# Linformer attention and a max-of-three FFN on one core: sums and AV in 64x32 array tiles, w rows permuted, six attention groups, stores on the Pool queue, first batch turned on TensorE

## Chip, cores, metric

One core of one Trainium2 chip. The metric is device time of the kernel in microseconds (us), the median of its runs. Most runs of one kernel agree within 0.3%. A trace gives the span (first to last instruction), which is about 1.8 us shorter than the time of the same run.

## The reference, cut

Eight batches, eight heads, 1024 positions, head size 64. Keys and values are projected from 1024 positions to 64 (E and F), softmax attention runs over these 64, and the result goes through an FFN whose hidden value is the maximum of three products.

```python
k_proj = np.einsum('ks,bhsd->bhkd', E, k)            # E: 64 x 1024
v_proj = np.einsum('ks,bhsd->bhkd', F, v)
scores = scale * np.matmul(q, k_proj.transpose(0, 1, 3, 2))
attn = np.exp(scores - max); attn = attn / (sum(attn) + 1e-09)
x = np.matmul(attn, v_proj)  # transposed and reshaped to (8192, 512)
h = np.maximum(np.maximum(x @ w1, x @ w2), x @ w3)   # 512 -> 768
out = h @ w_out                                      # 768 -> 512
```

## The kernel before

The FFN of batch b runs as one long stream on TensorE; the attention of batch b+1 is cut into groups that are put between the FFN's matmul groups at fixed places ("slots": a slot is one group of 4 matmuls of the first layer, or one of 6 of the second). The data moves like this: the Pool queue loads k, v, q of a batch (cast to bf16 on the way); the Sync (SP) queue turns q and the projected k (kp) by DMA transpose and also issues the stores of the output.

```python
NB = 2                                        # two buffers of k, v, q, qT, kp2, kpT
def load(b, src, dst):                        # two DMAs of 512 KB, Pool queue
    ...
def q_turn(b):
    nc.sync.dma_start_transpose(out=qT[b % NB]..., in_=q_t[b % NB]...)

def attention(b):
    def kv(lo, hi): ...                       # 16 matmuls 128x64, two column halves at once
    def kv_out():
        kv(SI // 2, SI)
        nc.scalar.copy(out=kp2[i][:, :, 0, :], in_=kv_k)
        nc.vector.tensor_copy(out=kp2[i][:, :, 1, :], in_=kv_k)
        nc.sync.dma_start_transpose(out=kpT[i], in_=kp2[i]...)
        ...                                   # two copies of v
    def scores(u): ...                        # 8 matmuls in 64x64 tiles, 2 exp of 128x1024
    def av(g):                                # two heads: 4 matmuls for sums, 4 for AV, 64x64 tiles
        ...
        nc.scalar.activation(out=lns[n2], in_=ps[:, AB + 2:AB + 4, :], func=AF.Ln)
        nc.scalar.activation(out=rinv[n2], in_=lns[n2], func=AF.Exp, scale=-1.0)
        nc.vector.tensor_tensor(out=xT[b % 3][:, g, :, :], in0=ps[:, AB:AB + 2, :], in1=rinv[n2]..., op=ALU.mult)
    # slots: kv 1 and 3, scores(0) 10, av(0) 14, av(1) 19, scores(1) 24, av(2) 29, av(3) 34

load(0, k, k_t); load(0, v, v_t); load(0, q, q_t)
...                                           # three w, w_out, on the Pool queue too
q_turn(0)
for _, g in attention(0): g()
load(1, k, k_t); load(1, v, v_t); load(1, q, q_t)
q_turn(1)
for b in range(B):
    if b + 2 < B:
        load(b + 2, k, k_t); load(b + 2, v, v_t); load(b + 2, q, q_t)
    for ch in range(2):
        ...                                   # 18 slots of layer 1; 4 slots of layer 2 of the half before,
                                              # a store on nc.sync after each second of these
    if b + 2 < B:
        q_turn(b + 2)
```

The loads of batch b+2 stand in loop b, but the Pool queue has nothing else to do. So it issues a load as soon as the buffer is free, which is when kv of the batch two before has read it. In loop b that starts the loads of batch b+3 right behind the kv of batch b+1.

The softmax here doesn't subtract the row's maximum and nothing guards it: scores larger than these inputs give would overflow.

## Time and profile before

| | before |
|---|---|
| time, median of 2 runs | 484.77 us |
| span of the profiled run | 481.2 us |
| TensorE busy, share of the span | 82% |
| first FFN matmul starts | 75.9 us |
| loop periods, loops 0 to 5 (first kv matmul to that of the next loop) | 49.1, 54.1, 52.5, 50.7, 52.1, 47.6 us |
| kpT, issue to landing (min/median/max) | 2.5/8.6/16.8 us |

First the page's slices, 40 of 12 us each: busy tenths of TensorE, its granted clock in tenths, busy tenths of the DMA engines, and what these moved.

```profile
PE   1300038699979999899979997999999999999996
PEclk9955557899988999899999998999999999999999
DMA  8999997941698046911696159815111511111122
GB/s 128 208 200 196 198 198 128 191 81 44 135 195 164 8 140 111 222 58 44 149 214 132 44 132 186 174 45 131 57 44 45 131 57 44 45 44 45 44 79 96
```

For the first six slices (72 us) TensorE is nearly idle and the DMA engines are full at about 200 GB/s. After that TensorE is nearly full, with dents in the slices where the DMA is busy.

The chain of waits, in order of time (start, duration, what), says what fills the first 75 us:

```profile
6.69 15.14 DMA q_t<-in_q_dram
21.91 19.61 SPq L74
41.58 16.78 DMA kpT<-kp
58.40 1.10 PE ps L113 x8
```

q of batch 0 lands at 21.8 us, the transpose of q then occupies the SP queue for 19.6 us, and only behind it the transpose of kp can go, which lands at 58.4 us. Then come 17 us of attention with nothing to overlap it.

In the loops: the timeline of loop 2 (start, duration, engine, line, operation, out<-in, count; in brackets the idle time before and what ended it).

```profile
184.82 1.48 POOL L71 DMA_DIRECT2D k_t<-in_k_dram  x2 [49.51 <-PE ps L90]
185.91 1.43 SPq L99 DMA_TRANSPOSE kpT<-kp  x1
...
194.66 1.02 PE L113 MATMUL ps<-qT,kpT 64*64 64x512 bf16 x8 [3.13 <-DMA kpT<-kp]
...
199.03 1.89 PE L156 MATMUL ps<-xT,w_sb 128*128 128x512 bf16 x7
...
200.85 0.41 PE L130 MATMUL ps<-pT,ones 64*64 64x512 bf16 x4
...
201.09 0.39 PE L130 MATMUL ps<-pT,vp 64*64 64x512 bf16 x4
...
201.41 1.04 PE L156 MATMUL ps<-xT,w_sb 128*128 128x512 bf16 x4
```

Two readings. The loads (184.82) begin just before the transpose of kp (185.91), which lands only at 194.6; the scores wait 3.13 us for it. And a group of eight tile matmuls takes from 200.85 to 201.41, 0.56 us, two slots of 0.2155 us (the spacing of the FFN's matmuls) and the rest switching; with 0.1 us ahead of it, 0.65 us.

The stall costs more than its idle time. The windows of 2 us over that stall (us; then busy time of PE, PEld, DVE, ACT, POOL with counts; granted clock, DMA share, GB/s):

```profile
192.00:194.00 2.00, 0.00 (x0) 0.00 (x0) 0.34 (x1) 0.00 (x0) 0.00 (x0) 1.00 1.20 191
194.00:196.00 2.00, 1.33 (x9) 0.28 (x10) 0.00 (x0) 0.27 (x1) 0.00 (x0) 0.69 1.16 248
196.00:198.00 2.00, 2.00 (x6) 0.76 (x5) 0.46 (x1) 1.67 (x2) 0.00 (x0) 0.50 1.14 267
```

After the idle time the clock is 0.50: six matmuls run in these 2 us, where eleven do at full clock (202 to 204 us of the same trace).

How slow the transpose of kp is, from the view of the tile kpT (durations on the queue, and issue to landing):

```profile
L99 SPq DMA_TRANSPOSE kpT<-kp x8: 1195/1467/6355, 41.6 to 388.7; - x8
DMA to landing us min/median/max: 2.5/8.6/16.8
```

The 2.5 us are of loops 5 and 6, in which no loads run any more, and these have no stall.

### The profile page before, as it was taken

The page shows a single profiled execution, that of the slowest core. Times are in us where ns is not written, and L with a number is a line of the kernel's source. Part 1 is how long each engine was busy: PE and PEld are TensorE (multiplying, and loading weights), DVE is VectorE, ACT ScalarE, POOL GpSimd, SP SyncE. Part 2 cuts the span into 40 slices and gives each one's busy share as a digit, 9 for nine tenths or more (in the row PEclk, how much of TensorE's full clock was granted, in tenths as well). Part 3 has the DMA queues.
Part 4 walks back from the last instruction along what each step waited for, and adds up shares of the span by engine and source line. Part 5 has one row for each costly group of instructions (what it writes and reads, how often), then busy time and mean ns, then how long its engine had stood idle before and what let it go on. Part 6 is the DMA issues. An engine that isn't in the chain of part 4 may idle for free.

```text
span 481.2 us, 5204 instructions
## 1 busy us (share of the span) xinstructions
PE 394.6 (82%) x2025; PEld 163.4 (34%) x2064; DVE 181.4 (38%) x243; ACT 197.3 (41%) x273; POOL 40.6 (8%) x60
## 2 busy tenths in 40 slices
PE   1300038699979999899979997999999999999996
PEld 1100012233423443344434442444444444344442
DVE  0100023354423554254425352454445444453331
ACT  1000064255435633455246623554465446542222
POOL 7311101200120003000200003000000000000000
PEclk9955557899988999899999998999999999999999
DMA  8999997941698046911696159815111511111122
GB/s 128 208 200 196 198 198 128 191 81 44 135 195 164 8 140 111 222 58 44 149 214 132 44 132 186 174 45 131 57 44 45 131 57 44 45 44 45 44 79 96
DMA packets 73977, 55.13 MB, mean 115 GB/s; under 512 B 38752, under 2 KB 65632, under 8 KB 73952
## 3 DMA queue, kind: packets, MB, share of 16 engines
q0 software_dynamic: 27872, 28.58, 36.1%
q1 hardware_dynamic: 46080, 26.22, 20.0%
q8 instruction: 16, 0.26, 0.2%
q14 instruction: 9, 0.07, 0.0%
HBM read 57.15 MB, written 16.78 MB: 154 GB/s over the span
## 4 chain that ended last, share of the span: by engine, by line
PE 73%; DMA 16%; SPq 4%; ACT 2%; DVE 2%; POOL 1%; issue 1%; DVEq 0%; POOLq 0%
PE ps L156 49%; PE ps L168 16%; DMA kpT<-kp 13%; SPq L74 4%; PE ps L130 4%; DMA q_t<-in_q_dram 3%; PE ps L88 3%; PE ps L113 2%; ACT pT L118 1%; DVE xT L136 1%; DVE kp L98 1%; ACT kp L97 1%; ACT rinv L135 0%; ACT lns L134 0%; POOL v_t L71 0%
## 5 line engine op out<-in xcount | busy, mean ns | idle before, releaser
L156 PE MATMUL ps<-xT,w_sb 128*128 128x512 bf16 x1127 | 269.2, 385 | 2.0 <-issue 0.5
L156 PEld LDWEIGHTS <-w_sb 128*128 128x128 bf16 x1152 | 110.2, 99 | 148.9 <-issue 25.8
L161 DVE TENSOR_TENSOR m<-ps,h1s 128x512 f32<-128x512 f32 x96 | 66.2, 690 | 114.7 <-PE ps L156 114.4
L168 PE MATMUL ps<-wo_sb,hT 128*128 128x512 bf16 x370 | 94.1, 385 | 0.7
L159 ACT COPY h1s<-ps 128x512 f32<-128x512 f32 x96 | 56.1, 584 | 61.8 <-PE ps L156 61.8
L136 DVE TENSOR_TENSOR xT<-ps,rinv 128x1024 bf16<-128x1024 f32 x32 | 39.2, 1225 | 109.5 <-ACT rinv L135 109.5
L163 DVE TENSOR_TENSOR hT<-ps,m 128x512 bf16<-128x512 f32 x96 | 66.3, 691 | 35.5 <-PE ps L156 27.6
L170 ACT COPY o_acc<-ps 128x512 f32<-128x512 f32 x64 | 37.4, 584 | 75.0 <-PE ps L168 74.8
L118 ACT ACTIVATE pT<-ps 128x1024 bf16<-128x1024 f32 x32 | 31.0, 1021 | 68.4 <-PE ps L113 68.4
L113 PE MATMUL ps<-qT,kpT 64*64 64x512 bf16 x128 | 12.2, 462 | 55.7 <-DMA kpT<-kp 54.3
L168 PEld LDWEIGHTS <-hT 128*128 128x128 bf16 x384 | 37.1, 99 | 49.5 <-issue 8.8
L134 ACT ACTIVATE lns<-ps 128x1024 f32<-128x1024 f32 x32 | 32.8, 1024 | 25.5 <-PE ps L130 25.5
L135 ACT ACTIVATE rinv<-lns 128x1024 f32<-128x1024 f32 x32 | 33.8, 1057 | 1.0
L71 POOL DMA_DIRECT2D k_t<-in_k_dram x16 | 11.9, 750 | 224.7 <-PE ps L90 213.1
L113 PEld LDWEIGHTS <-kpT 64*64 64x64 bf16 x128 | 2.6, 112 | 63.4 <-DMA kpT<-kp 57.7
L88 PE MATMUL ps<-k_t,eT 128*64 128x512 bf16 x64 | 19.1, 427 | 6.1 <-DMA k_t<-in_k_dram 6.1
L90 PE MATMUL ps<-v_t,fT 128*64 128x512 bf16 x64 | 18.9, 427 | 4.4 <-DMA v_t<-in_v_dram 4.4
L97 ACT CAST kp<-ps 64x512 bf16<-64x512 f32 x8 | 4.6, 579 | 41.8 <-PE ps L90 41.8
L130 PE MATMUL ps<-pT,ones 64*64 64x512 bf16 x128 | 14.0, 427 | 5.5 <-ACT pT L118 4.1
L130 PE MATMUL ps<-pT,vp 64*64 64x512 bf16 x128 | 13.5, 407 | 3.4 <-DVE xT L136 3.4
L98 DVE CAST kp<-ps 64x512 bf16<-64x512 f32 x8 | 5.5, 683 | 21.0 <-ACT kp L97 21.0
L71 POOL DMA_DIRECT2D q_t<-in_q_dram x16 | 12.1, 771 | 14.8 <-DMA qT<-q_t 8.1
(25 smaller groups left out, 53.5 us busy)
## 6 DMA issues: line engine op xcount, KB each, us to landing
out_dram<-o_acc SPq DMA_DIRECT2D x32, 512.0 KB, 2.7
k_t<-in_k_dram POOLq DMA_DIRECT2D x16, 512.0 KB, 8.4
v_t<-in_v_dram POOLq DMA_DIRECT2D x16, 512.0 KB, 13.0
q_t<-in_q_dram POOLq DMA_DIRECT2D x16, 512.0 KB, 16.6
w_sb<-in_moe_w_dram POOLq DMA_DIRECT2D x3, 768.0 KB, 21.8
wo_sb<-in_moe_w_out_dram POOLq DMA_DIRECT2D x1, 768.0 KB, 27.7
e_sb<-in_E_dram POOLq DMA_DIRECT2D x1, 128.0 KB, 3.1
f_sb<-in_F_dram POOLq DMA_DIRECT2D x1, 128.0 KB, 3.1
```

Source lines behind the costliest of these rows:

```text
L88: nc.tensor.matmul(out=ps[0:KP, AB, :], lhsT=eT[:, si, :], rhs=k_t[i][:, :, si, :], start=(si == 0), stop=(si == SI - 1))
L118: nc.scalar.activation(out=pT[:, 4 * u + 2 * h2:4 * u + 2 * h2 + 2, :], in_=ps[:, AB + 2 * h2:AB + 2 * h2 + 2, :], func=AF.Exp, scale=scale)
L130: nc.tensor.matmul(out=ps[col * D:(col + 1) * D, AB + 2 * (1 - what) + par, :], lhsT=ones[rows, :] if what == 0 else vp2[i][rows, h, :], r ...
L134: nc.scalar.activation(out=lns[n2], in_=ps[:, AB + 2:AB + 4, :], func=AF.Ln)
L135: nc.scalar.activation(out=rinv[n2], in_=lns[n2], func=AF.Exp, scale=-1.0)
L136: nc.vector.tensor_tensor(out=xT[b % 3][:, g, :, :], in0=ps[:, AB:AB + 2, :], in1=rinv[n2].rearrange("p (c n) -> p c n", c=2), op=ALU.mult)
L156: nc.tensor.matmul(out=ps[:, bank, :], lhsT=w_sb[i][:, ct, jt * P:(jt + 1) * P], rhs=xT[b % 3][:, ct, ch, :], start=(ct == 0), stop=(ct == ...
L159: nc.scalar.copy(out=h1s[jt % 2], in_=ps[:, bank, :])
L161: nc.vector.tensor_tensor(out=m12[jt % 2], in0=ps[:, bank, :], in1=h1s[jt % 2], op=ALU.max)
L163: nc.vector.tensor_tensor(out=hT[c % 2][:, jt, :], in0=ps[:, bank, :], in1=m12[jt % 2], op=ALU.max)
L168: nc.tensor.matmul(out=ps[:, bank, :], lhsT=hT[c % 2][:, jt, tt * P:(tt + 1) * P], rhs=wo_sb[:, jt, :], start=(jt == 0), stop=(jt == NJT - 1))
L170: nc.scalar.copy(out=o_acc[c % 2][:, tt, :], in_=ps[:, bank, :])
```

## The change

The intent: fewer TensorE and ACT passes in sums and AV (TensorE's array split into eight tiles of 64x32, four heads of one parity at once, so the sums of all heads are made once and two of four Ln/Exp pairs fall away; w's rows are permuted to fit the new order of x); six attention groups instead of eight; stores moved off the SP queue, and q's transpose moved into the middle of the loop, so that the transposes don't queue behind stores; the first batch's q and kp turned on TensorE to start the FFN earlier.

```diff
-    def attention(b):
+    def attention(b, turn):
...
-        groups.append((1, lambda: kv(0, SI // 2)))
-        groups.append((3, kv_out))
...
+        def quads(lhs):
+            for par in range(2):
+                for g in range(NPAIR):
+                    for u in range(2):
+                        rows = slice(u * KP, (u + 1) * KP)
+                        nc.tensor.matmul(out=ps[g * HD:(g + 1) * HD, AB + 2 * u + par, :],
+                                         lhsT=lhs(rows, g), rhs=pT[rows, g, par, :], start=True, stop=True,
+                                         tile_position=(u * KP, g * HD))
+        def sums():
+            quads(lambda rows, g: ones[rows, :])
+            ...                                  # 2 Ln and 2 Exp of 128x1024
+        def av(half):
+            quads(lambda rows, g: vp2[i][rows, g, half * HD:(half + 1) * HD])
+            ...                                  # 2 multiplications into xT
+        return [(2, kv), (10, lambda: scores(0)), (15, lambda: scores(1)), (20, sums),
+                (25, lambda: av(0)), (30, lambda: av(1))]
+    def turn_pe(i):                              # 8 transposes on TensorE, one copy
...
-            nc.sync.dma_start(out=out_v[b, ch]...
+            nc.gpsimd.dma_start(out=out_v[b, ch]...
...
-        nc.gpsimd.dma_start(out=wt, in_=w.rearrange("(ct p) j -> p ct j", p=P))
+        wv = w.rearrange("(j c p) n -> j p c n", j=NPAIR, c=NCT)
+        for j in range(NPAIR):
+            nc.gpsimd.dma_start(out=wt[j * HD:(j + 1) * HD], in_=wv[j])
...
-    q_turn(0)
-    for _, g in attention(0):
+    for h in range(H):                           # 32 transposes of 128x128 on TensorE, 8 copies
+        ...
+    for _, g in attention(0, turn_pe):
...
+            if slot == 16 and b + 2 < B:
+                q_turn(b + 2)
...
-        if b + 2 < B:
-            q_turn(b + 2)
```

More of the change, by code (lines that the diff above doesn't have):

```diff
@@ L25 @@
     NCT, NJT = DM // P, DF // P
+    NPAIR = H // 2
     scale = 1.0 / float(D) ** 0.5
@@ L37 @@
     ident = T([P, P], BF16, "ident")
-    ones = T([P, KP], BF16, "ones")
+    ones = T([P, D // 2], BF16, "ones")
     e_sb = T([KP, S], BF16, "e_sb")
@@ L52 @@
     kpT = [T([P, H, KP], BF16, f"kpT{i}") for i in range(NB)]
-    vp2 = [T([P, H, D], BF16, f"vp2_{i}") for i in range(NB)]
-    pT = T([P, H, 512], BF16, "pT")
+    vp2 = [T([P, NPAIR, D], BF16, f"vp2_{i}") for i in range(NB)]
+    pT = T([P, NPAIR, 2, 512], BF16, "pT")
     xT = [T([P, NCT, 2, 512], BF16, f"xT{i}") for i in range(3)]
@@ L80, with kv @@
     AB = 4
-    def attention(b):
+    HD = D // 2
+    def attention(b, turn):
         i = b % NB
-        groups = []
-        def kv(lo, hi):
-            for si in range(lo, hi):
+        def kv():
+            for si in range(SI):
                 nc.tensor.matmul(out=ps[0:KP, AB, :], lhsT=eT[:, si, :], rhs=k_t[i][:, :, si, :],
@@ L91, in kv @@
                                  start=(si == 0), stop=(si == SI - 1))
-        def kv_out():
-            kv(SI // 2, SI)
             kv_k = ps[0:KP, AB, :].rearrange("p (h d) -> p h d", d=D)
-            kv_v = ps[KP:P, AB, :].rearrange("p (h d) -> p h d", d=D)
+            kv_v = ps[KP:P, AB, :].rearrange("p (g par d) -> p g par d", par=2, d=D)
             nc.scalar.copy(out=kp2[i][:, :, 0, :], in_=kv_k)
             nc.vector.tensor_copy(out=kp2[i][:, :, 1, :], in_=kv_k)
-            nc.sync.dma_start_transpose(
-                out=kpT[i], in_=kp2[i].rearrange("p h c d -> p (h c d)"))
-            nc.scalar.copy(out=vp2[i][KP:P], in_=kv_v)
-            nc.vector.tensor_copy(out=vp2[i][0:KP], in_=kv_v)
@@ L104, in attention @@
-        groups.append((1, lambda: kv(0, SI // 2)))
-        groups.append((3, kv_out))
-        def scores(u):
-            hA, hB, hC, hD = range(4 * u, 4 * u + 4)
-            bank = {hA: AB, hB: AB + 1, hC: AB + 2, hD: AB + 3}
-            def mm(h, par, col):
-                r = slice(par * D, (par + 1) * D)
-                nc.tensor.matmul(out=ps[col * KP:(col + 1) * KP, bank[h], :], lhsT=kpT[i][r, h, :],
-                                 rhs=qT[i][r, h, :, :], start=True, stop=True)
-            mm(hA, 0, 0); mm(hC, 0, 1); mm(hD, 1, 0); mm(hB, 1, 1)
-            mm(hB, 0, 0); mm(hD, 0, 1); mm(hC, 1, 0); mm(hA, 1, 1)
-            for h2 in range(2):
-                nc.scalar.activation(out=pT[:, 4 * u + 2 * h2:4 * u + 2 * h2 + 2, :],
-                                     in_=ps[:, AB + 2 * h2:AB + 2 * h2 + 2, :], func=AF.Exp, scale=scale)
@@ L121, in attention @@
-        groups.append((10, lambda: scores(0)))
-        def av(g):
-            hA, hB = 2 * g, 2 * g + 1
-            for what in (0, 1):
-                for r in range(2):
-                    par = r if g % 2 == 0 else 1 - r
-                    rows = slice(r * KP, (r + 1) * KP)
-                    for col, h in ((0, hA), (1, hB)):
-                        nc.tensor.matmul(out=ps[col * D:(col + 1) * D, AB + 2 * (1 - what) + par, :],
-                                         lhsT=ones[rows, :] if what == 0 else vp2[i][rows, h, :],
-                                         rhs=pT[rows, h, :], start=True, stop=True)
-            n2 = g % 2
-            nc.scalar.activation(out=lns[n2], in_=ps[:, AB + 2:AB + 4, :], func=AF.Ln)
-            nc.scalar.activation(out=rinv[n2], in_=lns[n2], func=AF.Exp, scale=-1.0)
-            nc.vector.tensor_tensor(out=xT[b % 3][:, g, :, :], in0=ps[:, AB:AB + 2, :],
-                                    in1=rinv[n2].rearrange("p (c n) -> p c n", c=2), op=ALU.mult)
@@ L139, in attention @@
-        groups.append((14, lambda: av(0)))
-        groups.append((19, lambda: av(1)))
-        groups.append((24, lambda: scores(1)))
-        groups.append((29, lambda: av(2)))
-        groups.append((34, lambda: av(3)))
-        return groups
+            turn(i)
+            nc.scalar.copy(out=vp2[i][KP:P], in_=kv_v[:, :, 1, :])
+            nc.vector.tensor_copy(out=vp2[i][0:KP], in_=kv_v[:, :, 0, :])
+        def scores(u):
+            for gg in range(2):
+                g = 2 * u + gg
+                for par in range(2):
+                    r = slice(par * D, (par + 1) * D)
+                    for col in range(2):
+                        h = 2 * g + col
+                        nc.tensor.matmul(out=ps[col * KP:(col + 1) * KP, AB + 2 * gg + par, :],
+                                         lhsT=kpT[i][r, h, :], rhs=qT[i][r, h, :, :], start=True, stop=True)
+            for gg in range(2):
+                nc.scalar.activation(out=pT[:, 2 * u + gg, :, :], in_=ps[:, AB + 2 * gg:AB + 2 * gg + 2, :],
+                                     func=AF.Exp, scale=scale)
@@ new lines, in quads @@
+        def quads(lhs):
+            for par in range(2):
+                for g in range(NPAIR):
[6 more added lines that the diff above has]
+            quads(lambda rows, g: ones[rows, :])
+            for u in range(2):
+                nc.scalar.activation(out=lns[u], in_=ps[:, AB + 2 * u:AB + 2 * u + 2, :], func=AF.Ln)
+                nc.scalar.activation(out=rinv[u], in_=lns[u], func=AF.Exp, scale=-1.0)
@@ new lines, in av @@
+        def av(half):
+            quads(lambda rows, g: vp2[i][rows, g, half * HD:(half + 1) * HD])
+            for u in range(2):
+                nc.vector.tensor_tensor(out=xT[b % 3][:, 2 * u + half, :, :], in0=ps[:, AB + 2 * u:AB + 2 * u + 2, :],
+                                        in1=rinv[u].rearrange("p (c n) -> p c n", c=2), op=ALU.mult)
+        return [(2, kv), (10, lambda: scores(0)), (15, lambda: scores(1)), (20, sums),
+                (25, lambda: av(0)), (30, lambda: av(1))]
@@ L147, with turn_dma @@
+    def turn_dma(i):
+        nc.sync.dma_start_transpose(out=kpT[i], in_=kp2[i].rearrange("p h c d -> p (h c d)"))
+    def turn_pe(i):
+        for h in range(H):
+            nc.tensor.transpose(out=psb[:, AB + 1, h * KP:(h + 1) * KP],
+                                in_=kp2[i][:, h, :, :].rearrange("p c d -> p (c d)"), identity=ident[0:KP, 0:KP])
+        nc.vector.tensor_copy(out=kpT[i].rearrange("p h k -> p (h k)"), in_=psb[:, AB + 1, 0:H * KP])
     state = {"f": 0, "n": 0}
@@ L171, in down @@
         if tt % 2 == 1:
-            nc.sync.dma_start(out=out_v[b, ch][:, tt - 1:tt + 1, :], in_=o_acc[c % 2][:, tt - 1:tt + 1, :])
+            nc.gpsimd.dma_start(out=out_v[b, ch][:, tt - 1:tt + 1, :], in_=o_acc[c % 2][:, tt - 1:tt + 1, :])
     nc.scalar.preload_act_table_set("natural_log_exp_and_others")
@@ L191 @@
         nc.vector.tensor_copy(out=dst.rearrange("p si k -> p (si k)"), in_=psb[:, bank, :SI * KP])
-    q_turn(0)
-    for _, g in attention(0):
+    for h in range(H):
+        for s2 in range(SI // 2):
+            nc.tensor.transpose(out=psb[:, h % 4, s2 * P:(s2 + 1) * P],
+                                in_=q_t[0][:, h, 2 * s2:2 * s2 + 2, :].rearrange("p s d -> p (s d)"), identity=ident)
+        (nc.vector.tensor_copy if h % 2 else nc.scalar.copy)(
+            out=qT[0][:, h, :, :].rearrange("p s t -> p (s t)"), in_=psb[:, h % 4, 0:512])
+    for _, g in attention(0, turn_pe):
         g()
@@ L201 @@
     for b in range(B):
-        groups = attention(b + 1) if b + 1 < B else []
+        groups = attention(b + 1, turn_dma) if b + 1 < B else []
         if b + 2 < B:
```

## The prediction

> **What bounds the kernel now.** The chain of waits is 73% TensorE and 16% DMA. The windows show three parts.
>
> - Preamble: the first FFN matmul starts at 75.9 us. In the chain of waits, q of batch 0 lands at 21.8 us, its DMA transpose holds the queue 19.6 us, kp's transpose lands at 58.4 us, then 17 us of serial attention. DMA runs at 196 to 208 GB/s all that time (the slices).
> - Loops 0 to 4: each stalls at the first scores, waiting for kpT, because that transpose (8.5 to 9.1 us to landing) is issued 1.1 us after the loads of a later batch begin; without loads it takes 2.5 us. TensorE idles about 3.1 us, then runs at half clock for over 2 us (clock 0.50 in the windows). These loops last 50.7 to 54.1 us, loops without loads 47.7.
> - Otherwise: 192 FFN matmuls at 0.2155 us are 41.4 us; attention adds 6.2.
>
> **What the change does.**
>
> 1. AV and sums. Timeline: a group of 8 matmuls in 64x64 tiles stretches the FFN by 0.65 us (two slots of 0.216, the rest switching), four groups 2.6 us. After: three groups of 16 in eight tiles; if eight overlap, again two slots each, 1.95 us. The Trainium skill, "TensorEngine Tiling (Array Packing)", Tiling Modes, lists 64x32 as eight independent tiles and says that changing mode drains the array; the 0.1 to 0.2 us at each border here agrees. kv in one group saves one switch, 0.2. Sum: 0.9 us per loop, 6 over seven.
>
> 2. Preamble. Transposes on TensorE (estimate 4 us), kv, exp and normalization: first FFN matmul at about 46 us. But loop 0 then needs batch 1's kpT, behind its q transpose, behind q1, among the loads of batch 2. That is about 14 MB at 200 GB/s: estimate kpT1 at 73 to 76 us, where before it was 91.8. So TensorE stalls some 17 us at slot 10 of loop 0; of 30 us only about 18 remain.
>
> 3. Stores on the Pool queue. The Trainium skill, "DMA: Bandwidth & Descriptors", Issuing engines are not separate DMA queues, says moving them saves only issue time; but order matters: loads now stand behind the stores of the loop before. They start about 5 us before a loop's end, instead of at kv. The loads last about 20 us (q issued at 3 to 4 us, 16.6 to landing), so kpT, issued about 10 us in, still meets v and q. Its slack grows from 5.4 to 6.4 us: a stall of about 2 us remains in loops 1 to 5, less often with a cold clock. Gain about 2 us per loop.
>
> 4. w in pieces: hidden. Last stores through Pool: +1 us.
>
> **Sum.** Loop 1 starts at 106.5 instead of 125.7; six loops of 46.7 plus five stalls of 2.5; last loop 41.4, tail 11.5; 3.6 between span and time: 455 us. Range 444 to 468. Faster by over 2%: 0.95; same 0.04; slower 0.01.
>
> **What would show it.** AV groups of 16 in about 0.65 us of TensorE; first FFN matmul near 46 us; a wait for kpT of about 17 us in loop 0 ending near 74; loads starting before each loop's end; kpT still about 8 us to landing in loops 1 to 5, 2.5 in loop 6; loop 6 at 46.7.
>
> **What would make it wrong.** Tiles overlapping only four at a time (+9 us); kpT escaping the loads, or landing at their end (down to 443); loads delayed into the next kv.

## The result, and the profile after

The changed kernel takes 460.56 us (two runs, 460.56 and 460.57) against 484.77 us (484.32 and 485.22). The ratio is 0.9501, 95% interval 0.9460 to 0.9542. All experiments below are compared with the kernel before, run beside them on the same chip.

| | before | after |
|---|---|---|
| span | 481.2 us | 458.8 us |
| first FFN matmul | 75.9 us | 44.8 us |
| longest wait for kpT in loop 0 | 3.8 us | 17.4 us |
| loop periods, loops 0 to 5 | 49.1, 54.1, 52.5, 50.7, 52.1, 47.6 | 61.1, 49.0, 50.5, 51.5, 50.6, 48.9 us |
| loop without loads | 47.6 us | 46.7 us |

The slices of the page after:

```profile
PE   1165903999899989999799989999899999999994
PEclk9995875999999998999899998999999999999998
DMA  7999999018961498029941697029921111111022
GB/s 108 207 206 207 206 197 186 0 47 153 217 148 48 99 199 193 26 82 181 190 109 48 120 200 182 14 94 189 202 78 46 59 46 48 46 47 67 26 91 92
```

TensorE now works from the third slice on, but has a hole in the sixth, and the DMA is full until the end of the seventh. The timeline of the start says what the hole is:

```profile
20.90 1.89 PE L199 MATMUL ps<-ident,q_t 128*128 128x128 bf16 x16 [15.06 <-DMA q_t<-in_q_dram]
...
44.77 0.61 PE L159 MATMUL ps<-xT,w_sb 128*128 128x512 bf16 x1
...
54.63 17.44 SPq L75 DMA_TRANSPOSE qT<-q_t  x1
...
72.12 1.65 SPq L141 DMA_TRANSPOSE kpT<-kp  x1
...
75.81 1.07 PE L110 MATMUL ps<-qT,kpT 64*64 64x512 bf16 x8 [17.36 <-DMA kpT<-kp]
```

q of batch 0 is turned on TensorE at once (two bursts of 1.89 us) and the FFN starts 31 us earlier. But loop 0 holds the scores of batch 1, and their transposes are still DMA: q's occupies the queue for 17.4 us, kp's follows, and TensorE waits 17.36 us.

Loop 2 after:

```profile
154.36 1.53 POOL L72 DMA_DIRECT2D k_t<-in_k_dram  x2
...
162.87 1.20 SPq L141 DMA_TRANSPOSE kpT<-kp  x1
...
171.36 0.63 PE L110 MATMUL ps<-qT,kpT 64*64 64x512 bf16 x8 [2.00 <-DMA kpT<-kp]
```

The loads now start ahead of the loop, behind the last store of the loop before, and kp's transpose, issued 8.5 us later, still takes 8.5 us. The windows over that stall:

```profile
170.00:172.00 2.00, 0.64 (x9) 0.23 (x10) 0.16 (x1) 0.18 (x1) 0.00 (x0) 1.00 1.26 204
172.00:174.00 2.00, 2.00 (x6) 0.69 (x7) 0.58 (x1) 1.76 (x2) 0.00 (x0) 0.60 1.23 220
174.00:176.00 2.00, 2.00 (x7) 0.75 (x6) 0.11 (x1) 0.02 (x1) 0.00 (x0) 0.55 0.64 250
```

Again the clock falls, here after only 2.00 us of idle time. It fell in loops 2, 3 and 4 (idle 2.00, 3.05, 2.10 us) and not in loops 1 and 5 (2.21 and 2.13 us); the loops with the fall last 50.5 to 51.5 us, the others 49.0 and 48.9.

The traces show what goes with it. In each trace all changes of the granted clock lie on a grid of 3.41 us. The idle time of loop 1 (120.37 to 122.58 us) is cut in two by a line of the grid, that of loop 2 (169.36 to 171.36 us) lies within one step. Here are the step with most of the idle time and the step after it, first of loop 1, then of loop 2 (busy PE, and the clock after POOL):

```profile
121.19:124.60 3.41, 2.02 (x15) 0.84 (x16) 0.38 (x1) 1.55 (x2) 0.00 (x0) 1.00 1.25 205
124.60:128.02 3.42, 3.42 (x21) 1.40 (x18) 1.00 (x2) 1.55 (x3) 0.00 (x0) 1.00 1.05 228
168.98:172.39 3.41, 1.41 (x13) 0.38 (x12) 0.69 (x1) 0.76 (x2) 0.29 (x1) 1.00 1.25 203
172.39:175.80 3.41, 3.41 (x10) 1.21 (x9) 0.69 (x1) 1.37 (x2) 0.00 (x0) 0.50 0.96 251
```

The most idle time in one step is 1.39, 2.00, 2.69, 2.05 and 1.44 us in loops 1 to 5, and the clock fell after the three larger ones. In all traces of this case, between 82 us and the last matmuls, the clock fell 16 times, each time after a step with 2.00 us of idle time or more; after steps with up to 1.97 us it never fell, and after one of 2.01 (in the run with each tile group twice) it did not either. Ends of matmuls are modelled, so the border is known to some hundredths of a us at best. This is read from the records afterwards; no run moved the idle time against the grid.

A group of sixteen tile matmuls, and the FFN matmul after it:

```profile
138.38 0.63 PE L121 MATMUL ps<-pT,vp 64*32 64x512 bf16 x16
...
138.94 1.47 PE L171 MATMUL ps<-wo_sb,hT 128*128 128x512 bf16 x6
```

From 138.38 to 138.94 are 0.56 us: sixteen cost what eight did. And the tile view of kpT:

```profile
L141 SPq DMA_TRANSPOSE kpT<-kp x7: 1194/1195/1648, 72.1 to 364.3; - x7
DMA to landing us min/median/max: 2.6/8.5/9.5
```

Where the 22.4 us of span went, worked out from the timelines (a loop starts one FFN slot before its first kv matmul before the change, two after): loop 1 starts at 108.8 us instead of 125.6, 16.8 earlier. Loops 1 to 6 take 297.1 us instead of 304.5, 7.4 less; 6 x 0.9 = 5.4 of it is the shorter attention (46.7 against 47.6 in a loop without loads), about 2 is less stall (excess over the unstalled loop: 18.8 us in four loops before, 16.9 in five after). The end takes 1.9 us longer, all of it after the last matmul (4.2 us before, 6.1 after), with the last store on the Pool queue.

### The profile page after: what moved, and what is told of

Same layout as the page of the kernel before. It is cut to its first block, busy times and chain, and to the rows that moved or that the text cites. A ratio compares the mean times of both kernels' runs of the same rounds, so it can differ in the third digit from the quotient of the medians.

```text
span 458.8 us, 5527 instructions
## 1 busy us (share of the span) xinstructions
PE 393.9 (86%) x2232; PEld 166.9 (36%) x2232; DVE 180.3 (39%) x248; ACT 166.5 (36%) x245; POOL 68.0 (15%) x101
## 4 chain that ended last, share of the span: by engine, by line
issue 79%; POOL 10%; DMA 9%; POOLq 0%
POOL out_dram L175 5%; DMA q_t<-in_q_dram 4%; DMA w_sb<-in_moe_w_dram 3%; DMA v_t<-in_v_dram 2%; POOL v_t L72 2%; POOL q_t L72 2%; POOL k_t L72 1%; POOL wo_sb L190 0%; POOLq L265 0%; POOL f_sb L180 0%; POOL e_sb L179 0%; POOLq L175 0%; POOL ident masks.py:199 0%; POOL ident masks.py:197 0%; POOLq L72 0%
## 5 line engine op out<-in xcount | busy, mean ns | idle before, releaser
L171 PE MATMUL ps<-wo_sb,hT 128*128 128x512 bf16 x384 | 96.6, 390 | 0.0
L162 ACT COPY h1s<-ps 128x512 f32<-128x512 f32 x96 | 56.1, 584 | 81.7 <-PE ps L159 81.3
L175 POOL DMA_DIRECT2D out_dram<-o_acc x32 | 23.0, 718 | 358.5 <-ACT o_acc L173 333.4
L134 DVE TENSOR_TENSOR xT<-ps,rinv 128x1024 bf16<-128x1024 f32 x32 | 37.6, 1216 | 18.2 <-PE ps L121 18.2
L199 PE MATMUL ps<-ident,q_t 128*128 128x128 bf16 x32 | 3.8, 312 | 15.8 <-DMA q_t<-in_q_dram 15.8
L129 ACT ACTIVATE rinv<-lns 128x1024 f32<-128x1024 f32 x16 | 16.9, 1056 | 0.5
L91 PE MATMUL ps<-k_t,eT 128*64 128x512 bf16 x64 | 17.0, 414 | 0.0
L93 PE MATMUL ps<-v_t,fT 128*64 128x512 bf16 x64 | 17.0, 413 | 0.0
L128 ACT ACTIVATE lns<-ps 128x1024 f32<-128x1024 f32 x16 | 16.2, 1014 | 2.0 <-PE ps L121 2.0
L121 PE MATMUL ps<-pT,vp 64*32 64x512 bf16 x256 | 12.0, 410 | 4.5 <-ACT lns L128 2.5
L72 POOL DMA_DIRECT2D v_t<-in_v_dram x16 | 12.1, 772 | 3.6 <-DMA k_t<-in_k_dram 3.2
## 6 DMA issues: line engine op xcount, KB each, us to landing
q_t<-in_q_dram POOLq DMA_DIRECT2D x16, 512.0 KB, 16.9
```

The lines of the kernel that those rows point to most:

```text
L72: nc.gpsimd.dma_start(out=dst[b % NB][:, hs], in_=sv[:, hs])
L91: nc.tensor.matmul(out=ps[0:KP, AB, :], lhsT=eT[:, si, :], rhs=k_t[i][:, :, si, :], start=(si == 0), stop=(si == SI - 1))
L93: nc.tensor.matmul(out=ps[KP:P, AB, :], lhsT=fT[:, si, :], rhs=v_t[i][:, :, si, :], start=(si == 0), stop=(si == SI - 1))
L134: nc.vector.tensor_tensor(out=xT[b % 3][:, 2 * u + half, :, :], in0=ps[:, AB + 2 * u:AB + 2 * u + 2, :], in1=rinv[u].rearrange("p (c n) -> ...
L162: nc.scalar.copy(out=h1s[jt % 2], in_=ps[:, bank, :])
L171: nc.tensor.matmul(out=ps[:, bank, :], lhsT=hT[c % 2][:, jt, tt * P:(tt + 1) * P], rhs=wo_sb[:, jt, :], start=(jt == 0), stop=(jt == NJT - 1))
```

## The experiments

Two questions: is it really the loads that make the transposes late, in loop 0 and in loops 1 to 5; and what did each part of the change bring? The diffs are against the changed kernel unless another is named. An experiment's line numbers can differ by a few from those of the changed kernel.

### Loads held back until kpT has landed, loops 1 and up

A one-column copy on Pool that reads kpT stands ahead of the loads in the Pool queue, so the loads cannot start before kpT is there. Below it is called the gate.

```diff
-        if b + 2 < B:
+        if b + 2 < B and b < 1:
             load(b + 2, k, k_t); load(b + 2, v, v_t); load(b + 2, q, q_t)
...                                              # in the slot counter
+            if slot == 3 and b + 2 < B and b >= 1:
+                nc.gpsimd.tensor_copy(out=gate_t, in_=kpT[(b + 1) % NB][:, 0, 0:1])
+                load(b + 2, k, k_t); load(b + 2, v, v_t); load(b + 2, q, q_t)
```

> Changed kernel, but in loops 1 to 5 the loads of a later batch wait (a one-column copy on Pool that reads kpT) until kpT of that loop has landed. Theory (loads in flight make the transpose of kp slow, and the stall is its lateness plus the half clock after it): kpT lands 2.5 us after issue, no wait for it in loops 1 to 5, each of these loops 46.7 us instead of 49 to 51.5, time about 444 us. Rival (the transpose is slow by its own place in the queue, or the FFN waits for something else): kpT still about 8.5 us, loops as before, 460 us, or the waits come back as waits for late loads.

Measured: correct, 442.78 us (441.84 to 443.24), ratio to before 0.9142 (0.9120 to 0.9163). The view of kpT:

```profile
L142 SPq DMA_TRANSPOSE kpT<-kp x7: 1194/1194/1642, 71.6 to 346.4; - x7
DMA to landing us min/median/max: 2.6/2.6/3.8
```

kpT lands in 2.6 us, the waits of loops 1 to 5 are gone, and all these loops last 46.7 us. The late loads delay nothing. So the excess of loops 1 to 5 was wholly the transpose of kp among the loads, with what follows from it.

### The same in loop 0 too

```diff
-            if slot == 3 and b + 2 < B and b >= 1:
+            if slot == 3 and b + 2 < B:          # and no ungated load is left
```

> As e1, and the loads of batch 2 also wait for kpT of batch 1. Theory (in loop 0 the transposes of q1 and kp1 share the DMA engines with the loads of batch 2): the 17.4 us wait of loop 0 shrinks to about 4 us, the transpose of q1 lands about 7 us after q1 has landed, time about 431 us. Rival (the loop 0 wait comes from the late landing of q1 alone): it stays over 12 us, time about 440 us or more.

Measured: correct, 428.45 us (426.59 to 429.00), ratio 0.8841 (0.8815 to 0.8868). The wait of loop 0, and q's transpose of batch 1 in the view of the tile qT:

```profile
61.69 1.07 PE L111 MATMUL ps<-qT,kpT 64*64 64x512 bf16 x8 [3.97 <-DMA kpT<-kp]
```

```profile
L76 SPq DMA_TRANSPOSE qT<-q_t x1: 4787/4787/4787, 53.9 to 53.9; - x1
DMA to landing us min/median/max: 6.8/6.8/6.8
```

The wait fell from 17.4 to 4.0 us: q's transpose occupies its queue for 4.8 us instead of 17.4. The loads of batch 2 did that; the landing of q1 alone did not.

### And w_out loaded behind batch 1

```diff
-    nc.gpsimd.dma_start(out=wo_sb, in_=w_out...)     # ahead of the loads of batch 1
...
     load(1, q, q_t)
+    nc.gpsimd.dma_start(out=wo_sb, in_=w_out...)
```

> As e2, with the load of w_out moved behind the loads of batch 1 (first needed in the second half of loop 0). Theory (DMA throughput up to q1 sets the end of the rest of the wait): q1 lands about 4 us earlier, wait in loop 0 under 1 us, time about 427 us. Rival (something else holds kpT of batch 1): as e2.

Measured: correct, 424.76 us (424.35 to 425.09), ratio 0.8772 (0.8753 to 0.8790). No wait for kpT above 0.8 us is left; q's transpose of batch 1 starts at 49.9 instead of 53.9 us. What was left of loop 0's wait was the 0.8 MB of w_out ahead of q1.

### Matmuls put into the idle time

```diff
         def scores(u):
+            if u == 0 and 2 <= b <= 6:           # the scores of loops 1 to 5
+                for _ in range(9):
+                    nc.tensor.matmul(out=ps[:, AB + 3, :], lhsT=ident, rhs=w_sb[0][:, 0, 0:512], start=True, stop=True)
```

> Changed kernel with 9 matmuls of 512 columns (about 1.94 us, results unused) ahead of the first scores in loops 1 to 5, inside the idle time. Theory (three of the five stalls cost 1.6 us more because the clock falls to half after them): the stalls shrink to 0.1 to 1.1 us of idle time, kpT lands as before, no half clock, loops all about 49 us except the one with the 3 us wait at 50; time about 455.5 us. Rival (the excess of these loops isn't the clock): 460 us or more; if the fill only pushes the work back, 468.

Measured: correct, 456.11 us (455.19 to 456.67), ratio 0.9419 (0.9392 to 0.9446). Loops 1 to 5 last 49.1, 50.0, 48.9, 48.7, 48.9 us. The windows behind the longest remaining wait (1.33 us, loop 2):

```profile
172.00:174.00 2.00, 1.50 (x13) 0.61 (x14) 0.00 (x0) 1.03 (x2) 0.00 (x0) 1.00 1.24 205
174.00:176.00 2.00, 2.00 (x11) 0.92 (x10) 0.69 (x1) 1.47 (x2) 0.00 (x0) 1.00 1.07 312
```

The clock stays at 1.00. kpT is as late as before (median 8.5 us), so nothing was won in waiting; useless work made the kernel a little faster (ratio 0.9419 against 0.9501, intervals that don't touch) because the half clock after the wait is gone. This splits the cost of a stall: about 2.2 us of waiting, and about 1.7 us of slow clock in the loops that fall (in loop 2 of the changed kernel 50.46 - 46.70 - 2.00 = 1.76).

### Only the tiles, w rows and six groups

```diff
-            nc.gpsimd.dma_start(out=out_v[b, ch]...      # stores back on nc.sync
+            nc.sync.dma_start(out=out_v[b, ch]...
...                                              # q_turn(b + 2) back at the end of the loop
-    for h in range(H): ...                      # transposes of q on TensorE
-    for _, g in attention(0, turn_pe):
+    q_turn(0)
+    for _, g in attention(0, turn_dma):
```

> Changed kernel with the stores back on the SP queue, the q transpose back at the end of a loop and the first batch back on DMA transposes: only the tiles, the w rows and the six groups are left. Theory: 0.9 us per loop on TensorE, 1 us more slack for kpT in five loops, 3 us less attention before loop 0: about 470 us, 14 under the kernel before. Rival (tiles bring all the gain): 461; rival (tiles bring nothing on the critical path): 480 or more.

Measured: correct, 464.26 us, but in two groups (461.59, 461.64 and 466.88, 467.83), ratio 0.9610 (0.9540 to 0.9679). The size was a miss: more was won than 14 us. In the profiled run the span is 21.3 us shorter than before: 5.6 from the earlier start of loop 1, 5.5 from shorter loops, and 10.5 because the stalls of loops 1 to 5 shrank to 8.3 us from 18.8, with the stores still on the SP queue. The loop periods of the profiled run (461.59 us), loops 0 to 5, are 45.0, 46.7, 48.9, 48.8, 50.6, 46.7: loop 1 doesn't stall at all, and only one loop shows the length of a fallen clock. In loop 1 only one of the two halves of k had been issued when kp's transpose was (in loops 2 to 4 both), and kpT landed in time; why the second half was issued later is not settled. The two groups of times fit one or more clock falls, but only one run was profiled.

### The first batch back on DMA transposes

```diff
-    for h in range(H): ...
-    for _, g in attention(0, turn_pe):
+    q_turn(0)
+    for _, g in attention(0, turn_dma):
```

> Changed kernel with the first batch turned by DMA again. Theory (loop 0 is bound by kpT of batch 1, so most of the 30 us earlier start is lost in the 17 us wait): first FFN matmul at about 73 us, hardly any wait in loop 0, loop 1 starts near 114 instead of 108.8; time about 466 us, only 6 above the change. Rival (the earlier start is worth what it shows): 30 us or 17 us slower, 478 to 490.

Measured: correct, 470.28 us (469.44 to 471.40), ratio 0.9731 (0.9698 to 0.9764). First FFN matmul at 73.3 us, no wait in loop 0, loop periods 41.5, 48.4, 50.5, 50.5, 48.8, 53.3. So an FFN start 28.5 us later costs 10 us of time; the rest had been lost in the wait of loop 0. The theory holds, its size was 4 us short: kv of loop 1 starts 7.5 us later than in the changed kernel, and the last loop with loads happened to have a 3.7 us wait and a fallen clock.

### The stores back on the SP queue

```diff
-            nc.gpsimd.dma_start(out=out_v[b, ch]...
+            nc.sync.dma_start(out=out_v[b, ch]...
```

> Changed kernel with the stores back on the SP queue, so that loads start when kv has freed their buffers and not behind the stores. Theory (the queue of the stores matters only by when loads start; kpT meets loads either way): kpT 8.5 us to landing in loops 1 to 4, loops 49 to 51.5 us; loop 0's wait some us longer, since loads of batch 3 now join; time 461 to 466 us. Rival (moving the stores is worth several us in each loop): 470 or more.

Measured: correct, 463.16 us (462.97 to 464.16), ratio 0.9589 (0.9553 to 0.9625). Loop periods 71.8, 46.7, 48.8, 52.3, 50.6, 46.7. The SP queue in loop 0:

```profile
53.15 17.57 SPq L75 DMA_TRANSPOSE qT<-q_t  x1
70.78 6.40 SPq L141 DMA_TRANSPOSE kpT<-kp  x1
```

q's transpose lands at 85.5 us instead of 75.1, and kp's right behind it (it occupies the queue for 6.40 us instead of 1.65): loads of k and v of batch 3 now follow at 51 to 59 us. The wait of loop 0 grows from 17.4 to 28.6 us. Against that, loops 1 and 5 don't stall, loops 1 to 5 together are 5.4 us shorter, and the end is 1.7 us shorter. So the move of the stores is worth 2.6 us in all by the medians (about 4 by the ratios), and not through the stores: it holds the next loads back, which helps in loop 0 and brings stalls into loops 1 and 5.

### kp turned on TensorE in every loop

```diff
-            turn(i)
+            if turn is turn_dma or b == 0:       # loops call with turn=None
+                turn(i)
...
-        return [(2, kv), (10, lambda: scores(0)), ...
+        return [(2, kv), (6, (lambda: turn_pe(i)) if turn is None else (lambda: None)), (10, lambda: scores(0)), ...
```

> Changed kernel with kp turned on TensorE in every loop (its own group at slot 6), no DMA transpose of kp. Theory (loops 1 to 5 wait for nothing but kpT): no wait in them, about 0.6 us per loop for the transposes, loops 47.3 us, time about 448 us; loop 0 still waits some 16 us, now for qT of batch 1. Rival (q's transpose or loads would bind next in loops 1 to 5): a wait of 2 us stays there.

Measured: correct, 444.89 us (444.01 to 445.31), ratio 0.9202 (0.9172 to 0.9232). Loops 1 to 5 last 47.14 to 47.15 us without waits; loop 0 waits 15.3 us, now for qT. Taking the transpose off the DMA cures the loops as well as holding back the loads does, at 0.4 to 0.5 us per loop. Both ways of parting kpT and the loads give the same answer.

### Each tile group twice

```diff
         def sums():
+            quads(lambda rows, g: ones[rows, :])
             quads(lambda rows, g: ones[rows, :])
...
-            quads(lambda rows, g: vp2[i]...)
+            for _ in range(2):
+              quads(lambda rows, g: vp2[i]...)
```

> Changed kernel with every group of 16 tile matmuls of sums and AV issued twice (the second overwrites the first with the same values), so the result is the same. Theory (eight tiles overlap): three more groups of two 0.216 us slots, 1.3 us per loop and, at half clock, 2.6 us before loop 0: about 471 us. Rival (only four overlap at a time): twice that, 482 us.

Measured: correct, 472.11 us (466.63 to 473.32), ratio 0.9719 (0.9644 to 0.9795). The time agrees but scatters with the clock falls; the timeline is the better witness:

```profile
140.44 1.06 PE L121 MATMUL ps<-pT,vp 64*32 64x512 bf16 x32
141.43 1.47 PE L173 MATMUL ps<-wo_sb,hT 128*128 128x512 bf16 x5
```

32 matmuls take from 140.44 to 141.43, 0.99 us, where 16 took 0.56. So 16 more cost 0.43 us, two slots of 0.2155: eight run at once.

### q first in batch 0, and the groups of loop 0 later

On top of the version with the gate and w_out late:

```diff
+    load(0, q, q_t)
     load(0, k, k_t)
     load(0, v, v_t)
-    load(0, q, q_t)
...
+        late = 6 if b == 1 else 0                # slots of the five later groups of loop 0
```

> As e3, with q loaded before k and v in batch 0, so that the transposes of q overlap the loads of k and v, and with the five later attention groups of loop 0 moved 6 slots back. Theory (start bound by q's transposes after the last load): first FFN matmul about 41.5 us instead of 45.7, a wait under 2 us for kpT or v of batch 1; time about 421 us. Rival (loop 0 again bound by batch 1's data): 424 to 425 us.

Measured: correct, 422.46 us (422.03 to 422.64), ratio 0.8716 (0.8694 to 0.8737). First FFN matmul at 43.2 us instead of 45.7, no wait in loop 0 above 0.8 us. Somewhat less than expected: v, now last, lands at 22.3 us, and kv still runs at half clock behind it. It is the fastest version, 38 us under the change.

### The kernel before with nothing but the gate

Against the kernel before:

```diff
-        if b + 2 < B:
-            load(b + 2, k, k_t); load(b + 2, v, v_t); load(b + 2, q, q_t)
...
+            if slot == 4 and b + 2 < B:
+                nc.gpsimd.tensor_copy(out=gate_t, in_=kpT[(b + 1) % NB][:, 0, 0:1])
+                load(b + 2, k, k_t); load(b + 2, v, v_t); load(b + 2, q, q_t)
```

> The kernel before with only the loads held back until kpT has landed (the gate of e2), in all loops. Theory (the stalls of loops 0 to 4 were kpT among the loads): kpT 2.5 us to landing, loops 1 to 4 47.6 us instead of 50.7 to 54.1, loop 0 6 us shorter: about 458 us, as much as the whole change brought. Rival (the tiles and six groups are what shortens loops; the stalls come back elsewhere): 475 us or more.

Measured: correct, 459.89 us (459.45 to 460.27), ratio 0.9489 (0.9466 to 0.9513). The view of kpT:

```profile
L100 SPq DMA_TRANSPOSE kpT<-kp x8: 1194/1194/6357, 42.4 to 366.0; - x8
DMA to landing us min/median/max: 2.5/2.5/16.7
```

Loops 1 to 5 all last 47.6 us, loop 0 44.5 (the slow transpose that is left is that of batch 0). Holding back the loads in the old kernel brings as much as the whole change (0.9501), with neither tiles nor transposes on TensorE. It also gives the own worth of tiles and six groups without stalls: 47.6 against 46.7 us per loop. One caution with this trace: it holds no record of the granted clock before 81.3 us, and the views then read 1.00. Yet eight matmuls of scores take 1.07 us there, as in the kernel before at a recorded 0.50, against 0.63 us in the loops. The times of the matmuls are the safer reading.

## Why the prediction was right

The prediction was 455 us with a range of 444 to 468; measured were 460.56. Point by point:

1. **Tiles.** Predicted 0.65 us per group of 16 and a loop without loads at 46.7 us. Shown: 0.56 us plus the 0.1 at the border, two slots for 16 more, and loops of 46.7 us with stalls removed. The Trainium skill ("TensorEngine Tiling (Array Packing)", Tiling Modes) lists 64x32 as eight tiles that work independently; this trace agrees.
2. **Start.** Predicted first FFN matmul at about 46 us, then a wait of some 17 us at the first scores, kpT at 73 to 76. Measured 44.8, 17.4 and 75.8. That the loads of batch 2 make it so long is shown by holding them back (4.0 us). Of 31 us, 16.8 remained, not "about 18" to 19: loop 1 starts at 108.8, not 106.5.
3. **Loads against kpT.** Predicted loads before the loop's end, kpT still about 8 us, waits of about 2 us in loops 1 to 5. Measured 8.5 us and waits of 2.0 to 3.05. The cause is shown twice, by the gate and by turning kp on TensorE. The term that was mis-sized is "five stalls of 2.5": they cost 16.9 us in all, 3.4 each, because the clock fell in three of five loops; "less often with a cold clock" was right (before, it fell in four of five) and too little. The filling matmuls show that it is the clock. The words under this point were also too kind to the store queue: a gain of "about 2 us per loop" was written under it. With the stores put back, loops 1 to 5 are 5.4 us shorter, and the small gain in all comes from loop 0. The loops 1 to 6 became 1.2 us shorter each (7.4 in six), 0.9 of it by tiles and groups. The Trainium skill ("DMA: Bandwidth & Descriptors", Issuing engines are not separate DMA queues) says that choosing the issuing engine saves only issue time; the transfers here agree (a store took 2.7 us to land from the SP queue and 3.2 from the Pool queue), but the order on an engine's queue also decides when later transfers start (17.4 against 28.6 us of wait in loop 0).
4. **End.** Predicted +1 us for the last stores, measured 1.9 us after the last matmul. And 3.6 us were added from span to time, where both profiled runs show about 1.8 (482.93 us for the span of 481.2): the median of other runs had been compared with the profiled run's span.

The sum of the errors: +2.3 (loop 1 starts later), +4.4 (loops 1 to 5: 250.4 us, the sum of the exact periods, against 246.0), -1.8 (span to time), and +0.7 that the prediction's own sum was rounded down: the 5.6 us.

So the mechanism was right, and the number was helped a little by luck: the 1.8 us too many from span to time hid part of the 6.7 us that the two other terms were short. And the parts do not add. The prediction gave the first batch 18 us and the stores 2 us per loop, but undoing the first costs 10 us, undoing the second 2.6, and undoing both, with the place of q's transpose, 3.7 us by the medians (464.26 against 460.56, with times from 461.59 to 467.83). Each part changes where the stalls fall, and tiles and six groups alone bring some 20 of the 24 us.

What stays open: why kpT of 128 KB takes 8.5 us whenever loads run, early or late in them, is not split further; only that the loads cause it is shown. Why the stalls are so much smaller with tiles and six groups alone is not settled. No run undid the move of q's transpose by itself.

## What to carry to other kernels

A short transfer on the critical path that shares the DMA engines with bulk loads can be late by far more than its size (here 8.5 us instead of 2.6); let the bulk loads wait for it (a tiny operation on the loading queue that reads its result is enough) before making the computing engines faster. When a start is pulled earlier, look for the next transfer that it will run into: here 31 us of earlier start became 17. And after a stall look at the clock as well as at the idle time; 2.00 and 2.10 us of waiting cost 3.8 and 3.9.

## What the Trainium skill lacked or had wrong

- "DMA: Bandwidth & Descriptors", DMA Transpose (X-bar): has no time for a transpose beside loads, and where the skill gives a bandwidth for transposes it does not say what ran beside them. Measured: 128 KB in 2.6 us alone and 8.5 us beside loads; 1 MB in 6.8 us alone and 20.4 beside the loads of loop 0, with the queue occupied for 4.8 and 17.4 us.
- "DMA: Bandwidth & Descriptors", Issuing engines are not separate DMA queues: true of the bandwidth (no store became cheaper by the Pool queue: 3.2 us to land, 2.7 before), but silent on the order within an issuing queue. Moving the stores changed when loads start, and with it the wait of loop 0: 17.4 us against 28.6.
- "TensorE: Matmul & The Clock Gate", Why this matters for your kernels: advises against idle gaps over about 3 us. Here gaps of 2.00 and 2.10 us were followed by a clock of half, while 2.21 and 2.13 us were not; what told them apart was the idle time within one step of a 3.41 us grid (2.00 and 2.05 us against 1.39 and 1.44). Nine matmuls in the gap, with at most 1.33 us of it left idle, kept it at 1.00.
- "TensorEngine Tiling (Array Packing)": neither this page nor another gives a measured figure for 64x32. Here 16 matmuls of 512 columns cost 0.43 us in eight tiles, two slots of 0.2155, so all eight overlap, and a group inside a 128x128 stream cost 0.1 to 0.2 us more for the switch.
